# Attention scores as float32 products of 64 rows instead of products of split parts

## The chip, the cores and the metric

The kernel runs on one core of a Trainium2 chip. The metric is the time of one execution in device microseconds (us). A core has five engines that run side by side, each through its own list of instructions: TensorE (PE in the profile; its weight loads are PEld), VectorE (DVE), ScalarE (ACT), GpSimd (POOL) and SyncE (SP, which here only starts transfers). They wait for each other by semaphores. Products land in PSUM, eight banks of 512 float32 numbers on 128 partitions; PE, DVE and ACT reach it here.

## What is computed

Eight batches of eight heads, 576 tokens, 64 numbers per head. Half of the heads see a local window of 32 keys, the other half the keys at a distance of a multiple of 32. Then a feed-forward layer over all 4608 tokens, with weights that come as float64 numbers.

```python
scores = (1/8) * q @ k.T                     # per batch and head
rel = pos[:, None] - pos[None, :]
local   = (rel >= 0) & (rel < 32)            # heads 0 to 3
strided = (rel >= 0) & (rel % 32 == 0)       # heads 4 to 7
attn = softmax(where(mask, scores, -1e9))    # 1e-9 added to the sum
x = (attn @ v), heads side by side           # 4608 x 512
h = x @ w_in                                 # 512 x 2048
out = (h * clip(h + 3, 0, 6) / 6) @ w_out    # 2048 x 512
```

## The kernel before

**Pairs of heads.** Attention works on pairs of heads of one batch, 32 pairs in all, numbered 0 to 31 through the batches (four a batch: two local, two strided). The two heads of a pair lie on partitions 0 to 63 and 64 to 127 of one tile. A pair's steps are: load queries and keys (`qk`), transpose them by blocks on DVE (`t`), scores and softmax (`s`), transpose the probabilities and multiply by the values (`pv`), load the values (`v`).

**Blocks.** Local heads have six score blocks of 96 queries by 128 keys, strided heads five of 126 by 126; everything outside the blocks is masked anyway. So a local pair has 12 blocks and a strided pair 10.

**Two kinds of scores.** Pairs 0 to 7 (`PLAIN`) take the float32 transposes as they are and have float32 products (line 332): in pairs 0 to 3 over all 128 rows, with zeros in the place of the other head, in pairs 4 to 7 over the head's own 64 rows. These I call plain pairs. Pairs 8 to 31 split queries and keys in two float32r parts, a high part that ACT rounds (line 308) and a low part that DVE or POOL subtracts (line 309); DVE copies the keys' high part to the other half of the partitions (line 311). One product over 128 rows (line 334) then has the queries' high and low part against the keys' high part in its first columns and the high part against the keys' low part in the others. DVE adds the second columns to the mask (line 201), and then the first columns, with a running minimum (line 205). ACT takes the exponential (line 210), POOL divides by the sum (line 360).

**Banks.** A step of scores works on two blocks of one head and one bank, so a pair has six of them. Four banks (`w`) rotate among scores (`ps`), the second product of attention (`pv`) and the first product of the feed-forward (`ph`). The other four accumulate the second product of the feed-forward (`acc`).

**Second product of attention.** From pair 5 on DVE transposes the 32 by 32 blocks of the probabilities that can be other than zero (line 385), and line 411 multiplies, each head with 64 columns of the array.

**Feed-forward.** For each tile of 512 tokens and each of 16 chunks: 12 products into `ph` (lines 511 to 513), then ACT, DVE, ACT, POOL in a chain (lines 538, 539, 100, 101), and 12 products of the chunk before into `acc` (lines 494 to 496). The last 64 tokens of four batches make a tile of their own, `l`.

**Order.** The feed-forward of batch b is written with the attention steps of batch b + 1 spread evenly between its products; for the first two batches a string of steps gives the order. From that written order and a model of times a scheduler makes the list of each engine, with the chain at lines 538 to 101 at high priority. So a change of some steps moves other instructions too.

Of the kernel before, what the change touches and what calls it, by code (L numbers as in the profile page):

```python
# [8 lines left out]
F32 = mybir.dt.float32  # L9
# [18 lines left out]
NB = 3  # L28
VB = 1
PLAIN = 8  # L30
# [13 lines left out]
def attention_ffn(ctx: ExitStack, tc, q, k, v, w_in, w_out, out):  # L44
# [26 lines left out]
    # additive masks: local windows from PAD keys before the queries, strided blocks  # L71
# [19 lines left out]
    # They come as the words of float64 numbers (low, high) and are kept as two float32r parts, in  # L91
    # the same memory. The high word read as a float32 and scaled by 2**-112 has the float32
    # exponent and 20 bits of the mantissa three places to the right; the low word's top three
    # bits complete them.
# [8 lines left out]
    def weight_steps():  # L103
        """loads and conversions of parts of w_in (by rows) and w_out, in order of use"""
# [29 lines left out]
    def weights(loads, convs):  # L134
        """goes on to so many loads and conversions"""
        for todo, upto in ((wloads, loads), (wconvs, convs)):
            while todo and 8 * NQ - len(todo) < upto:
                todo.pop(0)()
# [6 lines left out]
    # the last tokens of four batches make a tile of their own  # L145
    left = [const.tile([P, NCC, B // 2 * LEFT], F32R, name=f"left{i}") for i in range(2)]

# [1 line left out]
    # Queries and keys come with 32 rows of tokens and half of a head's numbers on each quarter of  # L149
    # the partitions, so that transposes of 32 by 32 blocks give them by (head, number).  # L150
    # Scores of all but the first batches come from float32r parts: a head's queries' high part on
    # its own half of the partitions and the low part on the other, keys' high part on both beside
    # the low part on its own half. The first batches have float32 products.
    SR = [0, 7, 14, 21, STRIDE - RB]
    qk_plain, qk_split = [], []
# [12 lines left out]
    def split_k():  # L168
        if not qk_split:
            t = ap.tile([P, PAD + 4 * S], F32R, tag="kk", name="ksplit")  # L170
            nc.gpsimd.memset(t[:, :PAD].bitcast(F32), 0.0)
            for j in range(2):
                c0 = PAD + (2 * j + 1) * S
                nc.gpsimd.memset(t[D - D * j:P - D * j, c0:c0 + S].bitcast(F32), 0.0)
            qk_split.append(t)
        return qk_split[0]

    def keys(t, pad=0):
        """four parts of S keys; with pad, from so many columns before each part's first key"""
        return t[:, PAD - pad:PAD - pad + 4 * S].rearrange("p (a b s) -> p a b s", a=2, b=2)  # L180

    # probabilities of two heads, and their transposes, zero but for the 32 by 32 blocks that hold
    # allowed pairs
# [11 lines left out]
    def softmax(ps, mask, skip, e, mn, sm):  # L195
        """unnormalised exp of (ps + mask) over the last axis, into e; ps of several parts to add;
        the first block's first skip keys lie before all keys"""
        n, nb, w = e.shape
        m = mask.unsqueeze(1).to_broadcast([n, nb, w])
        if ps.shape[2] == 2:  # L200
            nc.vector.tensor_tensor(out=e, in0=ps[:, :, 1], in1=m, op=ALU.add)
            m = e
        for u in range(nb):
            c = slice(0 if u else skip, w)
            nc.vector.tensor_tensor_reduce(  # L205
                out=e[:, u, c], in0=ps[:, u, 0, c], in1=m[:, u, c], scale=-SCALE, scalar=BIG,
                op0=ALU.add, op1=ALU.min, accum_out=mn[:, u:u + 1])
# [8 lines left out]
    def bank(name):  # L216
        """a bank for what comes and goes; before the first tile those of the second product too"""
        nbank[0] += 1
        if before[0] and (early or nbank[0] % 2):
            acc = nbank[0] if early else nbank[0] // 2  # L220
            return pacc.tile([P, TOK], F32, tag=f"acc{acc % 4}", name=name)
        return pwk.tile([P, TOK], F32, tag="w", name=name)
# [41 lines left out]
    def pair_steps(b, c):  # L264
        """steps of one pair of heads: (loads, transposes, scores, probabilities, values)"""
# [11 lines left out]
        plain = b * NPAIR + c < PLAIN  # L277
# [17 lines left out]
        def t_split(x):  # L295
            def go():
                if x == "q":
                    d["qq"] = ap.tile([P, 2, S], F32R, tag="qq", name=f"qq{nm}")
                t = ap.tile([P, S], F32, tag="n", bufs=NB, name=f"{x}t{nm}")
                nc.vector.transpose(by_column(t), d[x])  # L300
                for j in range(2):
                    p, other = slice(D * j, D * j + D), slice(D - D * j, P - D * j)
                    if x == "q":
                        hi, lo = d["qq"][p, j], d["qq"][other, j]
                    else:
                        kt = keys(split_k())[:, j]
                        hi, lo = kt[p, 0], kt[p, 1]
                    nc.scalar.copy(hi, t[p])
                    (nc.vector, nc.gpsimd)[j if x == "q" else 1 - j].tensor_tensor(out=lo, in0=t[p], in1=hi.bitcast(F32), op=ALU.subtract)  # L309
                    if x == "k":  # L310
                        nc.vector.tensor_copy(kt[other, 0], hi.bitcast(F32))
            return go

        # score blocks of n queries and w keys; two share a bank
# [3 lines left out]
        k0 = q0 if loc else [x + PAD for x in q0]  # L318
        def s_step(j, i0):
            def go():  # L320
                blocks = range(i0, min(i0 + 2, nblk))
                ps = bank(f"ps{nm}{j}{i0}")
                np_ = 1 if plain else 2
                psv = ps[:n, :len(blocks) * np_ * w].rearrange("p (u t w) -> p u t w", u=len(blocks), t=np_)
                for u, i in enumerate(blocks):
                    pad = PAD if k0[i] < PAD else 0
                    kc = slice(k0[i] + pad - PAD, k0[i] + pad - PAD + w)
                    qc = slice(q0[i], q0[i] + n)
                    if plain:
                        own = slice(0, P) if padded else slice(D * j, D * j + D)  # L330
                        kt = keys(qk_plain[1], pad)[own, c % 2, j if padded else 0, kc]
                        nc.tensor.matmul(psv[:, u, 0], d["qt"][own, qc], kt, start=True, stop=True)
                    else:
                        nc.tensor.matmul(psv[:, u], d["qq"][:, j, qc], keys(split_k(), pad)[:, j, :, kc], start=True, stop=True)  # L334
                if i0 == 0:
                    if b * NPAIR + c < EARLY:
                        e = wp.tile([P, 6 * P], F32, tag=f"wo{NQ - 1}{c % 2 * 2 + j}", name=f"e{nm}{j}")
                    else:
                        if not es:
                            es.extend(ap.tile([P, 6 * P], F32, name=f"e{u}") for u in range(2))  # L340
                            for t in es:
                                nc.gpsimd.memset(t, 0.0)
                        e = es[j]
                    e = e[:, :nblk * P].rearrange("p (u w) -> p u w", u=nblk)
                    d["e", j] = e
                    if loc and b * NPAIR + c < EARLY:
                        nc.gpsimd.memset(e[:n, 0, :PAD], 0.0)
                    st = sp.tile([P, 2, 6], F32, tag="st", bufs=3, name=f"st{nm}{j}")
                    d["st", j] = st[:n, :, :nblk]
                e, st = d["e", j][:n, :, :w], d["st", j]  # L350
                sl = slice(i0, i0 + len(blocks))
                skip = PAD if loc and i0 == 0 else 0
                softmax(psv, mloc if loc else mstr, skip, e[:, sl], st[:, 0, sl], st[:, 1, sl])
                if i0 + 2 >= nblk:
                    sm = st[:, 1]
                    nc.vector.tensor_scalar_add(sm, sm, 1.0e-9)
                    nc.vector.reciprocal(sm, sm)  # L357
                    for bl, c0 in ((slice(0, 1), PAD), (slice(1, nblk), 0)) if loc else ((slice(0, nblk), 0),):
                        x = e[:, bl, c0:]
                        nc.gpsimd.tensor_tensor(out=x, in0=x, in1=sm[:, bl].unsqueeze(2).to_broadcast(x.shape), op=ALU.mult)  # L360
            return go

        where = {}

        def p_blocks(j):
            """transposes of the 32 by 32 blocks with allowed pairs"""
# [65 lines left out]
        ts = [(t_plain if plain else t_split)(x) for x in "qk"]  # L432
        ss = [s_step(j, i) for j in range(2) for i in range(0, nblk, 2)]
# [24 lines left out]
    def attention(b):  # L458
        """steps of one batch; the next pair's transposes stand between scores and probabilities"""
# [162 lines left out]
```

## Time and profile before

| | |
|---|---|
| runs | 1008.66 us median of 3 (1007.19 to 1011.6) |
| the profiled execution, first to last instruction | 1008.2 us |
| mean granted clock of TensorE | 0.978 of full speed |
| busy PE, DVE, ACT, POOL | 94%, 64%, 49%, 41% |
| transfers | 57.24 MB, most of it in the first 125 us |

In a row of grouped instructions stands the line, the engine, the operation, what is written and read, the shape, and the count. Behind it come the busy time, the mean duration in nanoseconds, and the idle time of the engine just before, with what ended it. A float32 product has two matmul records in the trace, a float32r product one. Durations of matmuls reach into each other, so what one adds is read from the starts. In a row of time order, "x4" says that four like records were merged, and the brackets give the idle time before and its end. "ps", "pv", "ph" and "acc" are the products named above, "ksplit" and "qq" the split keys and queries, "kplain" and "qplain" the plain ones.

### The profile page before, as it was taken

How to read it: one execution, taken by the hardware profiler on the slowest of the kernel's cores; microseconds unless marked ns; L12 is line 12 of the kernel's file. 1: busy time of each engine (PE TensorE's matmuls, PEld its weight loads, DVE VectorE, ACT ScalarE, POOL GpSimd, SP SyncE). 2: the span in 40 equal slices, each digit the busy share in tenths (PEclk: the TensorE clock that was granted, in tenths of full speed). 3: DMA queues.
4: the chain of work that ended last, by engine and by line, in shares of the span. 5: the costliest groups of instructions: out<-in, count | busy, mean ns of one | idle time of the engine just before them, and what ended most of it. 6: DMA issues, size and time to landing. Idle time of an engine off the chain costs nothing. (4 is left out here: it accounts for less than half of the span.)

```text
span 1008.2 us, 14965 instructions
## 1 busy us (share of the span) xinstructions
PE 948.7 (94%) x4848; PEld 765.7 (76%) x4848; DVE 648.0 (64%) x1869; ACT 489.3 (49%) x1346; POOL 412.2 (41%) x381
## 2 busy tenths in 40 slices
PE   5888898999999999999999999999899999999997
PEld 4665675778777778988787777778678878788896
DVE  7899999567777776126777777786766766311111
ACT  5676446455455444345554544555456445322232
POOL 4455566344434344225443444444434433222221
PEclk8898999899999999999999999999999999999999
DMA  7799400222222122103122311231213110100010
GB/s 149 160 283 295 91 14 16 58 61 37 37 58 63 30 38 45 43 1 60 34 38 46 77 27 36 38 79 27 41 32 77 33 25 14 42 1 1 1 42 21
DMA packets 207084, 57.24 MB, mean 57 GB/s; under 512 B 198304, under 2 KB 198304, under 8 KB 207008
## 3 DMA queue, kind: packets, MB, share of 16 engines
q1 hardware_dynamic: 207008, 56.31, 24.7%
q8 instruction: 38, 0.62, 0.3%
q14 instruction: 38, 0.31, 0.1%
HBM read 46.84 MB, written 9.44 MB: 56 GB/s over the span
## 5 line engine op out<-in xcount | busy, mean ns | idle before, releaser
L101 POOL TENSOR_TENSOR gl<-u,gh 128x512 fp32r<-128x512 f32 x128 | 170.4, 1333 | 241.8 <-ACT gh L100 223.3
L511 PE MATMUL ph<-xh,wi 128*128 128x512 f32 x512 | 209.4, 410 | 15.9 <-DVE u L539 8.2
L513 PE MATMUL ph<-xh,wi 128*128 128x512 f32 x512 | 205.0, 400 | 0.8 <-POOL wi L101 0.8
L512 PE MATMUL ph<-xl,wi 128*128 128x512 f32 x512 | 205.2, 401 | 0.4 <-DVE xl L428 0.4
L494 PE MATMUL acc<-wo,gh 128*128 128x512 f32 x512 | 201.9, 394 | 0.6 <-ACT gh L100 0.6
L495 PE MATMUL acc<-wo,gh 128*128 128x512 f32 x512 | 200.3, 391 | 0.0
L210 ACT ACTIVATE e<-e,st 126x126 f32<-126x126 f32 (+2 forms) x352 | 137.4, 392 | 92.2 <-DVE st L205 90.7
L496 PE MATMUL acc<-wo,gl 128*128 128x512 f32 x512 | 159.7, 395 | 0.0
L100 ACT CAST gh<-u 128x512 fp32r<-128x512 f32 x128 | 79.3, 619 | 161.6 <-DVE u L539 139.9
L539 DVE SCALAR_TENSOR_TENSOR u<-u,ph 128x512 f32<-128x512 f32 x128 | 86.4, 676 | 106.3 <-ACT u L538 105.5
L360 POOL TENSOR_TENSOR e<-e,st 96x96 f32<-96x96 f32 (+1 forms) x96 | 94.8, 1001 | 123.3 <-DVE st L357 104.3
L538 ACT ACTIVATE u<-ph,three 128x512 f32<-128x512 f32 x128 | 87.1, 681 | 92.7 <-PE ph L513 86.1
L511 PEld LDWEIGHTS ph<-xh,wi 128*128 128x128 f32 x512 | 98.6, 193 | 42.5 <-DVE u L539 11.0
L513 PEld LDWEIGHTS ph<-xh,wi 128*128 128x128 f32 x512 | 98.9, 193 | 23.4 <-POOL wi L101 1.4
L512 PEld LDWEIGHTS ph<-xl,wi 128*128 128x128 f32 x512 | 99.2, 194 | 19.5 <-DVE xl L428 1.3
L494 PEld LDWEIGHTS acc<-wo,gh 128*128 128x128 f32 x512 | 96.2, 188 | 21.5 <-ACT gh L100 1.2
L495 PEld LDWEIGHTS acc<-wo,gh 128*128 128x128 f32 x512 | 96.2, 188 | 18.2
L496 PEld LDWEIGHTS acc<-wo,gl 128*128 128x128 f32 x512 | 94.5, 188 | 20.3 <-POOL e L360 0.2
L385 DVE STREAM_TRANSPOSE atstr<-e 32x160 f32<-32x160 f32 x196 | 65.5, 334 | 8.4 <-POOL e L360 5.7
L205 DVE CUSTOM_DVE_ANT_0 e<-ps,e 96x128 f32<-96x128 f32 (+2 forms) x264 | 65.0, 280 | 2.4
L210 ACT ACTIVATION_READ_ACCUMULATOR e<-e,st 96x1 f32 (+1 forms) x352 | 66.2, 188 | 0.0
L385 DVE STREAM_TRANSPOSE atloc<-e 32x160 f32<-32x160 f32 (+1 forms) x156 | 56.5, 362 | 14.3 <-POOL e L360 12.3
(176 smaller groups left out, 1359.4 us busy)
## 6 DMA issues: line engine op xcount, KB each, us to landing
qn<-in_q_dram SPq DMA_DIRECT2D x128, 72.0 KB
kn<-in_k_dram SPq DMA_DIRECT2D x128, 72.0 KB
rawi<-in_moe_w_in_dram SPq DMA_DIRECT2D x16, 512.0 KB
rawo<-in_moe_w_out_dram SPq DMA_DIRECT2D x16, 512.0 KB
out_dram<-ob SPq DMA_DIRECT2D x32, 256.0 KB
vt<-in_v_dram SPq DMA_DIRECT2D x32, 160.0 KB
vt<-in_v_dram SPq DMA_DIRECT2D x160, 31.5 KB
out_dram<-obl SPq DMA_DIRECT2D x8, 128.0 KB
```

The lines of the kernel that those rows point to most:

```text
L101: eng.tensor_tensor(out=lo, in0=src, in1=hi.bitcast(F32), op=ALU.subtract)
L210: nc.scalar.activation(e[:, u, c], e[:, u, c], AF.Exp, bias=mn[:, u:u + 1], scale=-1.0, accum_out=sm[:, u:u + 1])
L360: nc.gpsimd.tensor_tensor(out=x, in0=x, in1=sm[:, bl].unsqueeze(2).to_broadcast(x.shape), op=ALU.mult)
L385: nc.vector.transpose(at[ks, i0:, qs], e[qs, i0:, ks])
L494: nc.tensor.matmul(acc[i], gh[:, sl], woh, start=fc == 0, stop=False)
L495: nc.tensor.matmul(acc[i], gh[:, sl], wol, start=False, stop=False)
L496: nc.tensor.matmul(acc[i], gl[:, sl], woh, start=False, stop=last)
L511: nc.tensor.matmul(ph, wih, xh[:, c], start=c == 0, stop=False)
L512: nc.tensor.matmul(ph, wih, xl[:, c], start=False, stop=False)
L513: nc.tensor.matmul(ph, wil, xh[:, c], start=False, stop=c == NCC - 1)
L538: nc.scalar.activation(u, ph, AF.Relu, bias=three)
L539: nc.vector.scalar_tensor_tensor(out=u, in0=u, scalar=6.0, in1=ph, op0=ALU.min, op1=ALU.mult)
```

## The change

All pairs are now like the plain ones 4 to 7 (pairs 0 to 3 stay over 128 rows). The split is gone, with its copies, subtractions and the addition at line 201. Query and key tiles of two pairs in turn lie in the two halves of the plain tiles. The first eight pairs (`FIRST`) keep their six score steps. From pair 8 on, four steps take their place: the first four blocks of both heads, in turn, into two banks and the softmax of the first head; the softmax of the second head; and the same for the remaining one or two blocks of each head. Comments that fell away are left out of the diff.

```diff
-PLAIN = 8
+FIRST = 8
...
     def softmax(ps, mask, skip, e, mn, sm):
         n, nb, w = e.shape
         m = mask.unsqueeze(1).to_broadcast([n, nb, w])
-        if ps.shape[2] == 2:
-            nc.vector.tensor_tensor(out=e, in0=ps[:, :, 1], in1=m, op=ALU.add)
-            m = e
         for u in range(nb):
             c = slice(0 if u else skip, w)
             nc.vector.tensor_tensor_reduce(
-                out=e[:, u, c], in0=ps[:, u, 0, c], in1=m[:, u, c], scale=-SCALE, scalar=BIG,
+                out=e[:, u, c], in0=ps[:, u, c], in1=m[:, u, c], scale=-SCALE, scalar=BIG,
...
-        def t_split(x):
-            def go():
-                if x == "q":
-                    d["qq"] = ap.tile([P, 2, S], F32R, tag="qq", name=f"qq{nm}")
-                t = ap.tile([P, S], F32, tag="n", bufs=NB, name=f"{x}t{nm}")
-                nc.vector.transpose(by_column(t), d[x])
-                for j in range(2):
...
-                    nc.scalar.copy(hi, t[p])
-                    (nc.vector, nc.gpsimd)[j if x == "q" else 1 - j].tensor_tensor(out=lo, in0=t[p], in1=hi.bitcast(F32), op=ALU.subtract)
-                    if x == "k":
-                        nc.vector.tensor_copy(kt[other, 0], hi.bitcast(F32))
-            return go
...
+        def scores(ps, j, i):
+            pad = PAD if k0[i] < PAD else 0
+            kc = slice(k0[i] + pad - PAD, k0[i] + pad - PAD + w)
+            own = slice(0, P) if padded else slice(D * j, D * j + D)
+            kt = keys(qk_plain[1], pad)[own, c % 2, j if padded else 0, kc]
+            nc.tensor.matmul(ps, d["qt"][own, q0[i]:q0[i] + n], kt, start=True, stop=True)
...
+        def s_both(i0, i1):
+            got = []
+            def mm():
+                blocks = range(i0, i1)
+                for j in range(2):
+                    ps = bank(f"ps{nm}{j}{i0}")
+                    got.append(ps[:n, :len(blocks) * w].rearrange("p (u w) -> p u w", u=len(blocks)))
+                for u, i in enumerate(blocks):
+                    for j in range(2):
+                        scores(got[j][:, u], j, i)
+                probabilities(got[0], 0, blocks)
+            def rest():
+                probabilities(got[1], 1, range(i0, i1))
+            return [mm, rest]
...
-        ts = [(t_plain if plain else t_split)(x) for x in "qk"]
-        ss = [s_step(j, i) for j in range(2) for i in range(0, nblk, 2)]
+        ts = [t_plain(x) for x in "qk"]
+        if b * NPAIR + c < FIRST:
+            ss = [s_step(j, i) for j in range(2) for i in range(0, nblk, 2)]
+        else:
+            ss = s_both(0, 4) + s_both(4, nblk)
```

What the scheduler makes of it is seen at two places. The first is TensorE's list at pair 13 (batch 3, a local pair; the digits in `ps_110` are the pair of the batch, the head, and the first block). Before, a stretch of products of one head stands between feed-forward products, here with two of the six steps (`ps_102` and `ps_114`) left out:

```order
L513 MATMUL ph_3_3105<-xh_1877,wi_580 128x512
L334 MATMUL ps_100_3156<-ksplit,qq_1_3018 96x256 x2
L494 MATMUL acc_0_2971<-wo_704,gh_2_3072 128x512
...
L494 MATMUL acc_2_2973<-wo_742,gh_3_3141 128x512
L334 MATMUL ps_104_3186<-ksplit,qq_1_3018 96x256 x2
L495 MATMUL acc_2_2973<-wo_742,gh_3_3141 128x512
...
L334 MATMUL ps_110_3211<-ksplit,qq_1_3018 96x256 x2
L334 MATMUL ps_112_3226<-ksplit,qq_1_3018 96x256 x2
L496 MATMUL acc_3_2974<-wo_742,gl_3_3142 128x512
```

Now (line 289 is the new place of line 332, lines 483 to 485 and 500 to 502 those of 494 to 496 and 511 to 513):

```order
L485 MATMUL acc_2_2884<-wo_704,gl_2_2951 128x512
L289 MATMUL ps_100_3034<-kplain,qplain 96x128
L289 MATMUL ps_110_3035<-kplain,qplain 96x128
...
L483 MATMUL acc_3_2885<-wo_704,gh_2_2950 128x512
...
L502 MATMUL ph_4_3056<-xh_1860,wi_902 128x512
L289 MATMUL ps_104_3078<-kplain,qplain 96x128 x2
L483 MATMUL acc_0_2882<-wo_742,gh_3_3019 128x512
...
L483 MATMUL acc_1_2883<-wo_742,gh_3_3019 128x512
L289 MATMUL ps_114_3079<-kplain,qplain 96x128 x2
L484 MATMUL acc_1_2883<-wo_742,gh_3_3019 128x512
```

The two rows ahead of the first "..." alternate four times, so eight blocks of both heads stand together; the last two blocks of each head stand in a place of their own, not beside the other head's.

The second place is DVE's list behind pair 12, from its softmax to that of pair 13 (`qq_1`, `ps_100` belong to pair 13, `qn_2` to pair 14). Before:

```order
L385 STREAM_TRANSPOSE atloc_1215<-e_1037 32x6x32 x4
L309 TENSOR_TENSOR qq_1_3018<-qt_1_3019,qq_1_3018 64x576
L385 STREAM_TRANSPOSE atloc_1215<-e_1037 32x6x32
L309 TENSOR_TENSOR ksplit<-kt_1_3034,ksplit 64x576
L311 CAST ksplit<-ksplit 64x576
L356 TENSOR_SCALAR st_01_2959<-st_01_2959 96x6
L300 STREAM_TRANSPOSE qt_2_3260<-qn_2_3049 128x18x32
L357 RECIPROCAL st_01_2959<-st_01_2959 96x6
L539 SCALAR_TENSOR_TENSOR u_2_3071<-u_2_3071,ph_2_3042 128x512
...
L201 TENSOR_TENSOR e_1037<-ps_100_3156,mloc 96x256
L205 ISA e_1037,st_10_3159<-ps_100_3156,e_1037 96x96
```

Now (lines 371, 528, 190 are 385, 539 and 205 of before; 272 and 276 are the transposes of queries and keys):

```order
L272 STREAM_TRANSPOSE qplain<-qn_2_2920 128x18x32
L276 STREAM_TRANSPOSE kplain<-kn_2_2925 128x18x32
...
L528 SCALAR_TENSOR_TENSOR u_1_2900<-u_1_2900,ph_1_2886 128x512
L371 STREAM_TRANSPOSE atloc_1215<-e_1037 32x5x32
L371 STREAM_TRANSPOSE atloc_1215<-e_1037 32x6x32 x5
...
L528 SCALAR_TENSOR_TENSOR u_2_2949<-u_2_2949,ph_2_2930 128x512
...
L190 ISA e_1037,st_10_3044<-ps_100_3034,mloc 96x96
```

The subtractions and the copy between the transposes of the probabilities are gone, and so is the addition ahead of the reductions.

More of the change, by code (lines that the diff above doesn't have):

```diff
@@ L154, in attention_ffn @@
     SR = [0, 7, 14, 21, STRIDE - RB]
-    qk_plain, qk_split = [], []
+    qk_plain = []
     def plain_q():
@@ L166, in plain_q @@
         return qk_plain[0]
[L168 to L171, printed above, removed]
-            for j in range(2):
[L173 to L176, printed above, removed]
     def keys(t, pad=0):
@@ L275, in vals @@
             d["v"] = load_v(b, c)
-        plain = b * NPAIR + c < PLAIN
         padded = b * NPAIR + c < KP
@@ L293, in t_plain @@
             return go
-        def t_split(x):
-            def go():
-                if x == "q":
-                    d["qq"] = ap.tile([P, 2, S], F32R, tag="qq", name=f"qq{nm}")
-                t = ap.tile([P, S], F32, tag="n", bufs=NB, name=f"{x}t{nm}")
-                nc.vector.transpose(by_column(t), d[x])
[L301 to L309, printed above, removed]
-                    if x == "k":
-                        nc.vector.tensor_copy(kt[other, 0], hi.bitcast(F32))
-            return go
         nblk = S // QB if loc else len(SR)
@@ L318, in pair_steps, with probabilities @@
         k0 = q0 if loc else [x + PAD for x in q0]
+        def scores(ps, j, i):
[4 more added lines that the diff above has]
+            nc.tensor.matmul(ps, d["qt"][own, q0[i]:q0[i] + n], kt, start=True, stop=True)
+        def probabilities(psv, j, blocks):
+            i0 = blocks[0]
+            if i0 == 0:
+                if b * NPAIR + c < EARLY:
+                    e = wp.tile([P, 6 * P], F32, tag=f"wo{NQ - 1}{c % 2 * 2 + j}", name=f"e{nm}{j}")
+                else:
+                    if not es:
+                        es.extend(ap.tile([P, 6 * P], F32, name=f"e{u}") for u in range(2))
+                        for t in es:
+                            nc.gpsimd.memset(t, 0.0)
+                    e = es[j]
+                e = e[:, :nblk * P].rearrange("p (u w) -> p u w", u=nblk)
+                d["e", j] = e
+                if loc and b * NPAIR + c < EARLY:
+                    nc.gpsimd.memset(e[:n, 0, :PAD], 0.0)
+                st = sp.tile([P, 2, 6], F32, tag="st", bufs=3, name=f"st{nm}{j}")
+                d["st", j] = st[:n, :, :nblk]
+            e, st = d["e", j][:n, :, :w], d["st", j]
+            sl = slice(i0, i0 + len(blocks))
+            skip = PAD if loc and i0 == 0 else 0
+            softmax(psv, mloc if loc else mstr, skip, e[:, sl], st[:, 0, sl], st[:, 1, sl])
+            if sl.stop == nblk:
+                sm = st[:, 1]
+                nc.vector.tensor_scalar_add(sm, sm, 1.0e-9)
+                nc.vector.reciprocal(sm, sm)
+                for bl, c0 in ((slice(0, 1), PAD), (slice(1, nblk), 0)) if loc else ((slice(0, nblk), 0),):
+                    x = e[:, bl, c0:]
+                    nc.gpsimd.tensor_tensor(out=x, in0=x, in1=sm[:, bl].unsqueeze(2).to_broadcast(x.shape), op=ALU.mult)
         def s_step(j, i0):
@@ L322, in go @@
                 ps = bank(f"ps{nm}{j}{i0}")
-                np_ = 1 if plain else 2
-                psv = ps[:n, :len(blocks) * np_ * w].rearrange("p (u t w) -> p u t w", u=len(blocks), t=np_)
+                psv = ps[:n, :len(blocks) * w].rearrange("p (u w) -> p u w", u=len(blocks))
                 for u, i in enumerate(blocks):
[L326 to L360, printed above, removed]
@@ L361, in s_step @@
-            return go
+                    scores(psv[:, u], j, i)
+                probabilities(psv, j, blocks)
+            return go
+        def s_both(i0, i1):
[12 more added lines that the diff above has]
+            return [mm, rest]
@@ L431, in pair_steps @@
         step = QB if loc else SB
-        ts = [(t_plain if plain else t_split)(x) for x in "qk"]
-        ss = [s_step(j, i) for j in range(2) for i in range(0, nblk, 2)]
+        ts = [t_plain(x) for x in "qk"]
+        if b * NPAIR + c < FIRST:
+            ss = [s_step(j, i) for j in range(2) for i in range(0, nblk, 2)]
+        else:
+            ss = s_both(0, 4) + s_both(4, nblk)
         groups = ([0, 1, 2], [3, 4, 5]) if loc else ([0, 1, 2, 3], [4])
```

## The prediction

> **What bounds the kernel now.** I read the page's engine row first, then the table of windows in three stretches (the start until the plain pairs are through, the stretch in which attention and feed-forward run side by side, and the tail), and then PE's waits in the second one. The columns of the table are length, busy time with instruction count of PE, PEld, DVE, ACT and POOL, then the granted clock and the DMA share.
>
> ```profile
> PE 948.7 (94%) x4848; PEld 765.7 (76%) x4848; DVE 648.0 (64%) x1869; ACT 489.3 (49%) x1346; POOL 412.2 (41%) x381
> 0.00:160.00 160.00, 129.08 (x683) 97.00 (x684) 145.85 (x371) 95.25 (x288) 85.84 (x93) 0.93 0.65 158
> 160.00:866.00 706.00, 683.16 (x3476) 552.73 (x3476) 481.84 (x1460) 353.21 (x982) 294.01 (x257) 0.99 0.20 41
> 866.00:1008.20 142.20, 136.50 (x693) 115.97 (x690) 20.36 (x38) 40.86 (x77) 32.37 (x32) 0.99 0.06 19
> ```
>
> The edited pairs, 8 to 31, all have their scores in the second stretch. PE, busy for 94% of the whole span, is busy there for 683.16 of 706 us, DVE for 481.84. The idle rest of PE is 706.00 - 683.16 = 22.84 us. The clock of 0.99 hides at most another 0.01 x 706 = 7 us of slow matmuls. So everything that PE could win from less loaded neighbours is about 30 us. What it waits for there, with total, count and longest:
>
> ```profile
> PE pv L411 <- issue: 9.6, 6, 2.2
> PE pv L411 <- DVE atloc L385: 5.5, 3, 2.5
> PE ph L511 <- DVE u L539: 5.1, 8, 3.6
> PE ph L511 <- DVE st L205: 1.7, 1, 1.7
> ```
>
> The reader is to see that all of it has DVE behind it: L411 needs DVE's block transposes L385, L511 a bank that DVE's L539 or L205 still reads. Even "issue" is such a case, as here, where PE idles 2.18 us until DVE's seven transposes end at 361.87 + 2.42 = 364.29:
>
> ```profile
> 361.87 2.42 DVE L385 STREAM_TRANSPOSE atstr<-e 32x160 f32<-32x160 f32 x7
> 364.39 0.52 PE L411 MATMUL pv<-atstr,vt 126*64 126x126 f32 x4 [2.18 <-issue]
> ```
>
> **What the change takes away.** These rows of the groups by shape name all of it (count, busy time, mean ns, idle time before):
>
> ```profile
> L309 POOL TENSOR_TENSOR ksplit<-kt,ksplit 64x576 fp32r<-64x576 f32 x24 | 36.7, 1529 | 64.4 <-ACT ksplit L308 36.1 <-PE ps L334 20.9 <-ACT gh L100 7.4
> L309 POOL TENSOR_TENSOR qq<-qt,qq 64x576 fp32r<-64x576 f32 x24 | 34.4, 1434 | 16.8 <-ACT qq L308 14.0 <-POOL e L360 1.6 <-POOL ksplit L309 0.8
> L311 DVE CAST ksplit<-ksplit 64x576 fp32r<-64x576 f32 x48 | 34.9, 728 | 2.8 <-ACT ksplit L308 1.2
> L308 ACT CAST ksplit<-kt 64x576 fp32r<-64x576 f32 x48 | 32.1, 669 | 12.2 <-PE ps L334 12.0
> L308 ACT CAST qq<-qt 64x576 fp32r<-64x576 f32 x48 | 32.1, 669 | 3.3 <-PE ps L334 1.9 <-PE ps L332 0.7
> L201 DVE TENSOR_TENSOR e<-ps,mloc 96x256 f32<-96x256 f32 x72 | 28.9, 418 | 30.3 <-PE ps L334 29.5
> L309 DVE TENSOR_TENSOR ksplit<-kt,ksplit 64x576 fp32r<-64x576 f32 x24 | 25.0, 1040 | 0.7
> L309 DVE TENSOR_TENSOR qq<-qt,qq 64x576 fp32r<-64x576 f32 x24 | 23.4, 976 | 1.1 <-ACT qq L308 0.4
> L201 DVE TENSOR_TENSOR e<-ps,mstr 126x252 f32<-126x252 f32 x48 | 19.7, 415 | 15.4 <-PE ps L334 15.0
> L201 DVE TENSOR_TENSOR e<-ps,mstr 126x126 f32<-126x126 f32 x24 | 6.9, 286 | 18.2 <-PE ps L334 18.1
> ```
>
> POOL loses 36.7 + 34.4 = 71 us, ACT 32.1 + 32.1 = 64, DVE 34.9 + 25.0 + 23.4 + 28.9 + 19.7 + 6.9 = 139. The transposes of queries and keys (L300, now as in L288 and L292) and the reductions L205 keep their number and size. None of these three engines sets the end, so the 274 us count only through the 30 us that PE waits. DVE's share in the stretch falls from 482 to about 343 of 706 us. I take 18 us as won back, three fifths: the waits behind a plain queue on DVE shrink, but the second product still stands behind softmax, POOL's multiplication and the transposes, and each score step now asks for two banks at once where it asked for one. The ends are 0 and 30.
>
> **What it adds to PE.** This is the term that decides. PE's rows, with start and duration: an old block of scores, a stretch of one new-style block (L332 has the same shapes in pairs 4 to 7), one of two blocks, and one in which blocks of both heads met. "xN" counts records; an L332 block has two of them, an L334 block one.
>
> ```profile
> 189.17 0.39 PE L495 MATMUL acc<-wo,gh 128*128 128x512 f32 x1
> 189.40 0.40 PE L334 MATMUL ps<-ksplit,qq 128*96 128x256 f32 x2
> 189.64 0.63 PE L496 MATMUL acc<-wo,gl 128*128 128x512 f32 x2
> ...
> 166.79 0.40 PE L513 MATMUL ph<-xh,wi 128*128 128x512 f32 x1
> 167.12 0.48 PE L332 MATMUL ps<-kplain,qplain 64*126 64x126 f32 x2
> 167.53 0.50 PE L511 MATMUL ph<-xh,wi 128*128 128x512 f32 x1
> 167.86 0.40 PE L512 MATMUL ph<-xl,wi 128*128 128x512 f32 x1
> ...
> 146.77 0.39 PE L513 MATMUL ph<-xh,wi 128*128 128x512 f32 x1
> 147.08 0.70 PE L332 MATMUL ps<-kplain,qplain 64*126 64x126 f32 x4
> 147.71 0.50 PE L494 MATMUL acc<-wo,gh 128*128 128x512 f32 x1
> 148.05 0.39 PE L495 MATMUL acc<-wo,gh 128*128 128x512 f32 x1
> ...
> 157.50 0.40 PE L494 MATMUL acc<-wo,gh 128*128 128x512 f32 x1
> 157.73 0.40 PE L495 MATMUL acc<-wo,gh 128*128 128x512 f32 x1
> 158.06 0.71 PE L332 MATMUL ps<-kplain,qplain 64*126 64x126 f32 x6
> 158.70 0.51 PE L513 MATMUL ph<-xh,wi 128*128 128x512 f32 x1
> ```
>
> Durations of matmuls overlap, so I go by starts. A feed-forward matmul takes 157.73 - 157.50 = 0.23 us. Two old blocks take 189.64 - 189.40 = 0.24, or 0.12 each, and the matmul ahead of them keeps its 0.23: they cost nothing beside themselves. One new block makes 167.86 - 166.79 = 1.07, less two ordinary steps of 0.23 that is 0.61. Two make 148.05 - 146.77 = 1.28, less 0.46 that is 0.82. The difference of 0.21 is two records: 0.11 each, and 0.61 - 0.22 = **0.39 us is a fixed price of each stretch**, half of it on the way in (167.12 comes 0.33 after 166.79), half on the way out and behind (167.86 comes 0.33 after 167.53). Six records with blocks of both heads took 158.70 - 157.73 = 0.97, no more than four alone (147.71 - 146.77 = 0.94): two of the six ran beside two others.
>
> The fixed price has a rule beside it: the Trainium skill, "TensorEngine Tiling (Array Packing)", Tiling Modes, says that changing the tiling mode, not just the tile, drains TensorE. The rows agree: 64 of 128 rows cost 0.39 per stretch, the 128-row L334 nothing.
>
> Now the count, in the order of the changed program. A mid pair has eight alternating blocks in one stretch, then the rest of each head in a stretch of its own, where the scheduler found the second bank free only later. Over the 24 pairs there are 264 blocks as before, in 73 stretches. With each record beside the other head's where the order lets them stand together, the 528 records need 374 places of 0.11. That is 374 x 0.11 + 73 x 0.39 = 41.1 + 28.5 = 69.6 us, against 264 x 0.12 = 31.7 before: **+38 us**. The second product, 64 columns wide, enters and leaves the same way. It is now cut into 75 stretches instead of 57, which is at most 18 x 0.39 = 7 us, but its heads alternate in more of them. I take +3, with ends 0 and 7.
>
> Nothing on PE covers this: in the stretch it has only those 30 us free. The first 160 us hold only pairs that stay plain, and their order is the same; the tail has no attention. Loads of queries and keys find their tiles free earlier, which at a DMA share of 0.20 is worth nothing.
>
> **Sum.** The profiled execution spans 1008.2 us, 0.5 under the median of the runs (1008.66, from 1007.19 to 1011.6), so I add to it directly: 1008.2 + 38 + 3 - 18 = **1031 us**. With nothing won back it is 1049, with all 30 us 1019.
>
> **Rivals.**
> *Heads do not overlap.* The 158.06 row is the only meeting of two heads' scores; its blocks went to two banks, as they now always do, which speaks for overlap. Against it: the order sometimes puts three blocks of a head in a row, and a late bank would part the two. With every record alone PE needs 528 x 0.11 + 28.5 = 86.6, so +55, and 1008.2 + 55 + 3 - 18 = 1048 us.
> *The fixed price is lateness, not a switch.* Then DVE's relief decides, and the kernel gets faster. If the 0.33 us steps at 167.12 and 167.53 came from weights or banks that were not ready, the lighter program would not pay them. PE would add 41.1 - 31.7 = 9 us, and with 18 to 30 won back the end is 987 to 999. It decides from the point where a stretch costs under 0.39 - (41 - 18) / 91 = 0.14 us, over 73 + 18 stretches. For it: both examples stand near semaphore waits. Against it: the two stretches show the same 0.39 to 0.01 us, at different places and with different neighbours. A half-way case (0.08 to 0.19) ends within 0.5% of before. The same page of the Trainium skill (Overview) promises up to twice the speed for a contraction of 64 and less. Taken alone that would make 264 places of 0.11, 29 us, 3 less than before; the rows of 146.77 and 166.79 speak against its being the whole bill.
>
> **Chances.** Forecast 0.70; no overlap, or waits for two banks of the same size, 0.17; the price not paid, fully or by half, 0.13. A change of under about 0.5% (5 us) can't be told from none here: faster 0.06, same 0.07, slower 0.87. The likeliest case has 1019 to 1042; to hold eight in ten I reach up through the serial case and a little below the full win-back: 1016 to 1050.
>
> **What would show it.** In the new profile the score line should have 528 records of about 0.27 us on 64 rows, from pair 8 on, many starting within 0.01 us of another of the other head; the step into each stretch should be 0.33 us and not 0.23. PE's instruction count rises by 264. PE must stay above 95% busy between 160 us and the end of attention, with DVE under 50%, and that stretch must be longer by some 23 us while the first 160 us and the tail stay. If L411's waits on DVE are gone and the stretch is still longer, the terms are right. If PE's idle time grows past 30 us, banks are the cause that I underrated; if the steps into stretches are 0.23, the fixed price was wrong, and so is the sign.

## The result, and the profile after

The changed kernel takes **1022.4 us** (median of four runs, 1021.84 to 1024.39) against 1008.5 us in the same comparison: 1.0131 times the time before, 95% interval 1.0104 to 1.0157. It is slower, as forecast, by 14 us where the forecast had 22; the time lies in the stated range.

The profiled execution spans 1020.1 us. The page's engine row, and the windows in the same three stretches as before (the second ends with the last attention work, now about 876 us):

```profile
PE 977.9 (96%) x5112; PEld 764.1 (75%) x5112; DVE 509.5 (50%) x1629; ACT 430.5 (42%) x1250; POOL 335.5 (33%) x330
0.00:160.00 160.00, 127.24 (x670) 96.52 (x671) 147.34 (x365) 93.99 (x283) 83.91 (x92) 0.93 0.66 162
160.00:876.00 716.00, 712.30 (x3747) 550.14 (x3746) 342.71 (x1230) 295.46 (x892) 218.73 (x207) 1.00 0.19 40
876.00:1020.10 144.10, 138.36 (x699) 117.49 (x697) 19.49 (x35) 41.09 (x75) 32.86 (x32) 0.99 0.06 19
```

DVE, ACT and POOL lost about what was counted (DVE 648.0 to 509.5, ACT 489.3 to 430.5, POOL 412.2 to 335.5: 139, 59 and 77 us, for 139, 64 and 71). PE's records rose by 264 to 5112. In the middle stretch PE's idle time fell from 22.84 to 716.00 - 712.30 = 3.70 us, and the clock is full, but the stretch is 10 us longer (the prediction had some 23): PE has more to do, and nothing else sets the time there. What it still waits for in that window:

```profile
PE pv L397 <- DVE u L528: 1.5, 1, 1.5
PE ph L500 <- DVE u L528: 1.3, 1, 1.3
PE pv L397 <- DVE st L190: 0.6, 1, 0.6
PE acc L483 <- ACT gh L100: 0.3, 1, 0.3
```

Now PE's rows around pair 13 in time order, first the stretch with eight blocks of both heads in turn, then the two with the rest of each head:

```profile
322.47 0.39 PE L485 MATMUL acc<-wo,gl 128*128 128x512 f32 x1
322.79 1.12 PE L289 MATMUL ps<-kplain,qplain 64*96 64x128 f32 x16
323.83 0.50 PE L483 MATMUL acc<-wo,gh 128*128 128x512 f32 x1
324.17 0.40 PE L484 MATMUL acc<-wo,gh 128*128 128x512 f32 x1
...
327.18 0.39 PE L502 MATMUL ph<-xh,wi 128*128 128x512 f32 x1
327.50 0.67 PE L289 MATMUL ps<-kplain,qplain 64*96 64x128 f32 x4
328.10 0.50 PE L483 MATMUL acc<-wo,gh 128*128 128x512 f32 x1
328.44 0.40 PE L484 MATMUL acc<-wo,gh 128*128 128x512 f32 x1
```

The 16 records took 324.17 - 322.47 = 1.70, less two ordinary steps of 0.23 that is 1.24 us: eight places of 0.11 and 0.36. The four records of one head took 328.44 - 327.18 - 0.46 = 0.80: four places of 0.11 and 0.36. So both heads' records do run beside each other, and the second, short stretch pays a fixed price as large as that of the long one.

I summed this over all score stretches from pair 8 on, from the start of the matmul ahead to the second one behind, less two ordinary steps: 73 stretches, 528 records in 364 places, **67.0 us**. The 264 old blocks at 0.12 come to 31.7.

### The profile page after: what moved, and what is told of

Its sections match the earlier page's. It is cut to its first block, busy times and chain, and to the rows that moved or that the text cites. A ratio compares the mean times of both kernels' runs of the same rounds, so it can differ in the third digit from the quotient of the medians.

```text
span 1020.1 us, 15024 instructions
## 1 busy us (share of the span) xinstructions
PE 977.9 (96%) x5112; PEld 764.1 (75%) x5112; DVE 509.5 (50%) x1629; ACT 430.5 (42%) x1250; POOL 335.5 (33%) x330
## 4 chain that ended last, share of the span: by engine, by line
PE 83%; DVE 9%; SPq 4%; DMA 2%; ACT 1%; issue 1%; POOL 0%; DVEq 0%; ACTq 0%
PE acc L483 12%; PE ph L500 11%; PE acc L484 11%; PE acc L485 11%; PE ph L501 10%; PE ph L502 10%; PE ps L289 5%; PE pv L397 4%; SPq L224 2%; PE phl L500 1%; PE phl L502 1%; PE phl L501 1%; PE accl L483 1%; PE accl L484 1%; PE accl L485 1%; DVE fo L123 1%
## 5 line engine op out<-in xcount | busy, mean ns | idle before, releaser
L101 POOL TENSOR_TENSOR gl<-u,gh 128x512 fp32r<-128x512 f32 x128 | 168.2, 1315 | 443.6 <-ACT gh L100 414.3
L483 PE MATMUL acc<-wo,gh 128*128 128x512 f32 x512 | 207.6, 406 | 0.3 <-ACT gh L100 0.3
L484 PE MATMUL acc<-wo,gh 128*128 128x512 f32 x512 | 201.0, 393 | 0.0
L485 PE MATMUL acc<-wo,gl 128*128 128x512 f32 x512 | 174.2, 394 | 0.0
L500 PEld LDWEIGHTS ph<-xh,wi 128*128 128x128 f32 x512 | 96.8, 189 | 38.2 <-DVE u L528 5.0
L318 POOL TENSOR_TENSOR e<-e,st 96x96 f32<-96x96 f32 (+1 forms) x96 | 92.0, 976 | 79.7 <-DVE st L315 59.4
L502 PEld LDWEIGHTS ph<-xh,wi 128*128 128x128 f32 x512 | 97.6, 191 | 22.7 <-POOL wi L101 1.4
L289 PEld LDWEIGHTS ps<-kplain,qplain 64*96 64x96 f32 (+3 forms) x704 | 67.9, 180 | 45.9 <-issue 34.2
L289 PE MATMUL ps<-kplain,qplain 64*96 64x128 f32 (+3 forms) x704 | 87.6, 296 | 13.9 <-DVE kplain L276 10.7
L414 DVE TENSOR_TENSOR xl<-pv,xh 128x288 fp32r<-128x288 f32 (+1 forms) x64 | 33.4, 526 | 93.2 <-ACT xh L413 93.1
L190 DVE CUSTOM_DVE_ANT_0 e<-ps,mloc 96x96 f32<-96x96 f32 (+1 forms) x192 | 43.5, 276 | 71.9 <-PE ps L289 71.8
```

The costliest lines, as they stand in the source:

```text
L101: eng.tensor_tensor(out=lo, in0=src, in1=hi.bitcast(F32), op=ALU.subtract)
L289: nc.tensor.matmul(ps, d["qt"][own, q0[i]:q0[i] + n], kt, start=True, stop=True)
L483: nc.tensor.matmul(acc[i], gh[:, sl], woh, start=fc == 0, stop=False)
L484: nc.tensor.matmul(acc[i], gh[:, sl], wol, start=False, stop=False)
L485: nc.tensor.matmul(acc[i], gl[:, sl], woh, start=False, stop=last)
L500: nc.tensor.matmul(ph, wih, xh[:, c], start=c == 0, stop=False)
```

## The experiments

All times are medians. Each set was run beside the kernel before, whose medians were 1009.77, 1009.04 and 1010.44 us in the three sets; ratios are to it.

### The price of 64 rows against the price of float32

The first kernel has all pairs over 128 rows, with zeros in the place of the other head, as pairs 0 to 3 have it.

```diff
-KP = 4
+KP = 32
```

> Edit: all pairs lie as pairs 0 to 3 do, each head's queries and keys over 128 rows with zeros in the place of the other head; the products stay float32, the order of steps stays. Heads can no longer overlap. Theory (the fixed price of a stretch, 0.39 us, belongs to blocks on 64 of the 128 rows): no fixed price for scores, 528 records of 0.11 us one after the other, about 58 us in place of the 67 us that the changed kernel's trace shows for its score stretches, so about 9 us faster than the changed kernel, near 1013 us. Rival (the price belongs to the change between float32r and float32 products): 58 + 73 x 0.39 = 86 us, so about 19 us slower, near 1041 us. DVE gets one transpose of 1.0 us more per pair, 24 us in all, which should hide.

Measured: 1012.38 us, ratio 1.0030 (1.0011 to 1.0048). PE's rows, with the same four records of one head's last blocks:

```profile
324.06 0.39 PE L502 MATMUL ph<-xh,wi 128*128 128x512 f32 x1
324.29 0.60 PE L289 MATMUL ps<-kplain,qplain 128*96 128x128 f32 x4
324.64 0.49 PE L483 MATMUL acc<-wo,gh 128*128 128x512 f32 x1
324.97 0.39 PE L484 MATMUL acc<-wo,gh 128*128 128x512 f32 x1
```

324.97 - 324.06 - 0.46 = 0.45 us: four places of 0.11 and nothing besides; the step into the stretch is 0.23. The products are float32 and stand between float32r ones, so the type carries no price. Doubling the rows, half of them zeros, is 10 us faster than the changed kernel. From pair 8 on, the score stretches sum to 58 us in place of 67. The edit also pads pairs 4 to 7, and 1.8 of the 10 us stand already ahead of pair 8: the 351st feed-forward matmul, with 392 attention records ahead of it in both traces, starts at 179.0 us in place of 180.8. Whether that is the padding or a difference between two executions was not separated.

The reverse needs the type kept and the rows halved. The next two kernels start from the kernel before and leave out the low parts of queries and keys (their places hold zeros, so the scores are those of rounded numbers). The first shows the relief of DVE and POOL by itself, with PE's products as before; the second differs from it only in the rows.

```diff
                     nc.scalar.copy(hi, t[p])
-                    (nc.vector, nc.gpsimd)[j if x == "q" else 1 - j].tensor_tensor(out=lo, in0=t[p], in1=hi.bitcast(F32), op=ALU.subtract)
-                    if x == "k":
-                        nc.vector.tensor_copy(kt[other, 0], hi.bitcast(F32))
...
-                softmax(psv, mloc if loc else mstr, ...)
+                softmax(psv[:, :, :1], mloc if loc else mstr, ...)
```

> Edit: the kernel before, with the low parts of queries and keys left out: their halves are set to zero once, the subtractions, the copy of the keys' high part and the addition ahead of the reductions are gone, so the scores are products of the rounded high parts alone. PE has the same products as before. DVE loses about 139 us and POOL 71 us, ACT keeps its copies. Theory (the relief is worth the stalls of PE, some 23 of 27 us, less a few more stretches of the second product): about 18 to 22 us faster than before, near 988 us. Rival (DVE's relief is worth little, the changed kernel's gain came from elsewhere): within 5 us of before.

```diff
-                        nc.tensor.matmul(psv[:, u], d["qq"][:, j, qc], keys(split_k(), pad)[:, j, :, kc], start=True, stop=True)
+                        own = slice(D * j, D * j + D)
+                        nc.tensor.matmul(psv[:, u], d["qq"][own, j, qc], keys(split_k(), pad)[own, j, :, kc], start=True, stop=True)
```

> Edit: as the kernel with the low parts left out, but each product uses only the head's own 64 rows; still float32r, still one record of 256 columns per block. The rest is the same. Theory (the price belongs to 64 rows): the order has about 134 stretches of scores, so 134 x 0.39 = 52 us slower than the kernel with the low parts left out, near 1040 us, and steps of 0.33 us into each stretch. Rival (the price belongs to float32 beside float32r, or to lateness): no difference, near 988 us, steps of 0.23 us.

Measured: the relief alone 986.58 us, ratio 0.9764 (0.9725 to 0.9804); with 64 rows 1036.38 us, ratio 1.0258 (1.0216 to 1.0300). The window of the first from 160 us to the end of its attention shows where the relief went, 690.00 - 687.33 = 2.67 us of idle PE:

```profile
160.00:850.00 690.00, 687.33 (x3514) 554.28 (x3513) 353.04 (x1226) 355.55 (x991) 220.62 (x209) 1.00 0.21 43
```

A score stretch of the second in time order:

```profile
323.53 0.39 PE L512 MATMUL ph<-xh,wi 128*128 128x512 f32 x1
323.85 0.47 PE L333 MATMUL ps<-ksplit,qqhi 64*96 64x256 f32 x2
324.25 0.50 PE L510 MATMUL ph<-xh,wi 128*128 128x512 f32 x1
324.59 0.39 PE L511 MATMUL ph<-xl,wi 128*128 128x512 f32 x1
```

324.59 - 323.53 - 0.46 = 0.60 us, of which two places of 0.12; the rest, 0.36, is the fixed price, now with float32r throughout. The two kernels differ by 49.8 us; over 134 stretches that is 0.37 us each. With the rule of the Trainium skill, "TensorEngine Tiling (Array Packing)", Tiling Modes (a change of the tiling mode drains TensorE), this agrees: the price came with 64 rows in either type, and went with 128.

The weight loads (PEld) show what is late in such a step. Here is the first load of the stretch above, and below it that of the 128-row stretch at 324.29 us in the kernel with all pairs over 128 rows:

```profile
323.85 0.24 PEld L333 LDWEIGHTS ps<-ksplit,qqhi 64*96 64x96 f32 x2 [0.35 <-issue]
...
324.06 0.61 PEld L289 LDWEIGHTS ps<-kplain,qplain 128*96 128x96 f32 x4
```

The 64-row load starts together with its matmul (323.85), the 128-row load 0.23 us ahead of its own (324.06 against 324.29). From 200 us on this is so at each of the 131 entries into a score stretch of the 64-row float32r kernel, at each of the 69 of the changed kernel, and at each way out: 1 to 2 ns from the load's start to the matmul's, where the load of a 128-row stretch starts at least 0.22 us ahead. So the next weights are not loaded under the running matmul when the rows change. Whether PE drains, or only holds the load back, these rows do not separate.

### What taking both heads in turn is worth

```diff
-FIRST = 8
+FIRST = 32
```

> Edit: the changed kernel, but all pairs keep the six score steps of one head each, two blocks in one bank; 64 rows, float32. Heads hardly meet. Theory (0.39 us per stretch plus 0.11 us per record that runs alone): the order has 135 stretches of scores, so 528 x 0.11 + 135 x 0.39 = 58 + 53 = 111 us in place of 67, about 43 us slower than the changed kernel, near 1065 us. Rival (taking both heads in turn is worth little, the loss came from the new order and the banks): within 10 us of the changed kernel.

Measured: 1066.14 us, ratio 1.0560 (1.0508 to 1.0612). So with 64 rows, the steps of both heads together save 44 us against the old steps. The sum over its stretches, made as above, is 135 stretches, 528 places, 110.5 us against 67.0: 164 places more, at 0.11 some 18 us, are the overlap that is lost, and the rest goes with 62 stretches more.

### Half rows where the heads meet, whole rows elsewhere

This and the last kernel keep the keys padded, and use 64 rows only for the four alternating blocks.

```diff
-KP = 4
+KP = 32
...
-            own = slice(0, P) if padded else slice(D * j, D * j + D)
+            own = slice(0, P) if padded and not half else slice(D * j, D * j + D)
...
-                        scores(got[j][:, u], j, i)
+                        scores(got[j][:, u], j, i, half=i0 == 0)
```

> Edit: keys with zeros for the other head as in the 128-row kernel, but the first four blocks of both heads use 64 rows, in turn, and the remaining one or two blocks of each head use all 128 rows. Theory (0.39 us only for stretches with 64-row blocks, records of both heads overlap only there): in the order 42 us of places, and 32 stretches with the price (106 of both kinds less 74 of the second product), 42 + 32 x 0.39 = 55 us in place of 67, so about 12 us faster than the changed kernel, near 1010 us. Rival (overlap is worth nothing beyond the price): as the 128-row kernel or slower, 1012 us and more.

Measured: 1008.00 us, ratio 0.9989 (0.9966 to 1.0012): 14 us faster than the changed kernel, and no difference from before that can be told. Its score stretches sum to about 54 us in place of 67; here too pairs 4 to 7 are padded.

### The same price in the second product

The second product uses 64 of the array's 128 columns, and a row of the changed kernel's trace has its fixed price too:

```profile
314.53 0.39 PE L484 MATMUL acc<-wo,gh 128*128 128x512 f32 x1
314.85 0.38 PE L397 MATMUL pv<-atloc,vt 128*64 128x96 f32 x2
315.16 0.50 PE L500 MATMUL ph<-xh,wi 128*128 128x512 f32 x1
315.50 0.39 PE L501 MATMUL ph<-xl,wi 128*128 128x512 f32 x1
```

One block alone: 315.50 - 314.53 - 0.46 = 0.51 us. The scheduler often lets the first head's first block run ahead by itself, since the other head's transposes come later. Taking the second head first holds the block back until both are there.

```diff
-                    for j in range(2):
+                    for j in (1, 0):
                         a = where[j, i][:, skip:]
```

> Edit: in the changed kernel the second product of attention takes the pair's second head first, so that its first matmul waits for the later of the two sets of transposes and the rest can follow at once. Theory (a stretch of 64-column matmuls has the same fixed price as one of 64-row blocks): the order has 58 stretches of the second product in place of 75 and 78 of scores in place of 73, and about 3 us fewer places; 17 x 0.39 + 3 - 5 x 0.39 = 8 us faster than the changed kernel, near 1014 us, if PE's waits for the transposes do not grow. Rival (columns have no such price): 3 us faster at most.

> Edit: the same turn of the two heads in the second product, in the kernel before. Theory: the order has 30 stretches of the second product in place of 57 and about 8 us fewer places; 27 x 0.39 + 8 = 19 us faster than before if PE's waits stay, near 990 us; they may grow by some us, since PE then waits with less behind it. Rival (columns have no such price): 8 us faster at most.

Measured: 1020.63 us in the changed kernel, ratio 1.0120 (1.0093 to 1.0147), and 1007.39 us in the kernel before, ratio 0.9987 (0.9972 to 1.0003). Both expectations missed: 2 us where 8 were expected, and under 2 where 19 were. In the kernel before, the stretches did shrink. Their sum from 186 us on fell from 69.0 us in 56 stretches (waits inside them counted) to 35.4 in 30. But a new wait took most of the gain. The next feed-forward product may have been placed for an earlier end of its chain, which no run shows; PE's waits in the middle window:

```profile
PE acc L494 <- ACT gh L100: 26.0, 21, 3.4
PE acc L496 <- POOL gl L101: 0.7, 4, 0.2
```

In the changed kernel the same wait stands in the first 190 us, in the window from 60 us on:

```profile
PE acc L483 <- ACT gh L100: 12.3, 4, 5.2
PE acc L485 <- POOL gl L101: 2.3, 3, 1.0
```

By the work done, PE is 2.7 us behind there: the 401st feed-forward matmul, with 432 attention records ahead of it in both traces, starts at 200.8 us in place of 198.1. The granted clock between 100 and 135 us is lower too, 0.80 in place of 1.00, so waits and slow matmuls were not told apart. From there to the end the turned kernel wins back 5 us. So the turn was tried from pair 8 on only:

```diff
+                    for j in ((1, 0) if b * NPAIR + c >= 8 else (0, 1)):
```

> Edit: the changed kernel, with the heads of the second product turned only from pair 8 on. Theory (a stretch of 64-column matmuls costs 0.39 us): 60 stretches in place of 75, 2.8 us fewer places, and 78 stretches of scores in place of 73; 15 x 0.39 + 2.8 - 5 x 0.39 = 7 us faster than the changed kernel, near 1015.5 us. Rival (columns have no such price): 2 us faster at most.

Measured: 1017.90 us, ratio 1.0085 (1.0056 to 1.0114), 4.5 us faster than the changed kernel, between theory and rival. The stretches of the second product, 57 in place of 73 behind the first tile, sum to 45.8 in place of 54.1 us, and the score stretches rose from 67.0 to 69.9: 5.4 us less in all. The profiled execution is shorter by only 3.4 us: it is 1.9 us late already at its 51st feed-forward matmul (71.5 against 69.6 us), ahead of every pair that the edit turns, so that difference is not the edit's. The two turned kernels differ in the first eight pairs alone, and in time by 1020.63 - 1017.90 = 2.7 us. The gain of 8.3 us in the product itself holds places and stretches together, so a price per column stretch is only read from rows like the one above: 0.51 less two places of 0.08, about 0.35 us. The 0.08 is estimated from the last kernel below, where a stretch with four places more takes 0.33 us more from its first start to that of the next matmul.

### All of it together

```diff
+                ps = None
                 for j in range(2):
-                    ps = bank(f"ps{nm}{j}{i0}")
-                    got.append(ps[:n, :len(blocks) * w].rearrange("p (u w) -> p u w", u=len(blocks)))
+                    if i0 == 0 or ps is None:
+                        ps = bank(f"ps{nm}{j}{i0}")
+                    c0 = 0 if i0 == 0 else j * len(blocks) * w
+                    got.append(ps[:n, c0:c0 + len(blocks) * w].rearrange("p (u w) -> p u w", u=len(blocks)))
```

This is added to half rows where the heads meet and to the turned heads: the last blocks of both heads now share one bank. First with the heads turned in all pairs, then from pair 8 on.

> Edit: the kernel with 64 rows for the first four blocks and 128 for the rest, with the heads of the second product turned, and the last blocks of both heads in one bank. Theory: 25 us of places and 50 stretches for the second product (44.5 us in place of 58.8), 43 us of places and 33 stretches for scores (56 us in place of 67), so about 25 us faster than the changed kernel, near 997 us. Rival (columns have no such price): the scores' 11 us and 3 us of places, near 1008 us.

> Edit: the kernel with half rows first, last blocks of both heads in one bank and the heads of the second product turned, but turned only from pair 8 on. Theory (the turned heads in the first eight pairs cost the 9.7 us by which their first tile ended later, 203.7 against 194.0 us; from there on stretches cost 0.39 us each): 51 stretches of the second product and 34 of 64-row scores as before, the first tile back at about 194 us, near 997 us. Rival (the turn itself costs waits anywhere, the first pairs are no special place): within 3 us of 1005.65.

Measured: 1005.65 us, ratio 0.9969 (0.9953 to 0.9984), and **997.59 us**, ratio 0.9879 (0.9849 to 0.9909). The second is faster than the kernel before and than the changed kernel. These two combined kernels differ only in the turn in the first eight pairs, which is the 8 us between them: at the 401st feed-forward matmul the first is 8.1 us behind (204.2 against 196.1 us, 432 attention records ahead in both). (The 203.7 and 194.0 us of the last expectation are the starts of the first copy out of the first tile's banks, in the first of these and in the changed kernel, and not the tile's end.) The windows of the second up to and past the middle stretch:

```profile
160.00:852.00 692.00, 687.04 (x3729) 550.97 (x3730) 365.05 (x1243) 292.14 (x887) 216.43 (x205) 1.00 0.20 41
852.00:996.30 144.30, 138.36 (x699) 117.50 (x697) 19.56 (x35) 41.21 (x75) 32.95 (x32) 1.00 0.06 19
```

The score stretches sum to 55.2 us and those of the second product to 42.1, against 67.0 and 54.1 in the changed kernel: 24 us, as the time has it (1022.4 - 997.6 = 25). What the shared bank is worth was not run alone. Against the kernel with half rows where the heads meet (1008.00 us), the gain of 10 us is found in the second product (some 55 to 42 us); its scores, at about 54 us, were no longer than these.

## Why the prediction was right

**The sign and its reason** were right. PE set the time of the middle stretch, the 274 us taken from the other engines counted only through PE's waits, and the fixed price of a stretch was real.

**Scores on PE:** +38 was forecast, 67.0 - 31.7 = +35 came. The count of stretches (73) was exact. 364 places came for 374 counted, so the order was read as costing a little more than it did. The fixed price was 0.36 to 0.39 us. Float32 and float32r at 64 rows have it and both at 128 rows do not, so it belongs to the rows.

**Second product:** +3 was forecast, from 57 to 75 stretches. The sum over them is 58.8 us after. Before, waits stand inside them, so the clean sum is only estimated, at some 55 from the same places and price: no contradiction, but not a measurement either.

**Won back from waits:** this was the term that was mis-sized. 18 us of 30 were forecast as won back, "three fifths", on the ground that the second product would still stand behind softmax and transposes and that each step would want two banks. PE's idle time fell by 22.84 - 3.70 = 19.1 us, and the clock rose from 0.99 to 1.00. Gap by gap (each start beyond its ordinary step, slow-clock matmuls too) the lost time from 170 us on was 27.3 us before and is 4.1 now: 23. The kernel with the relief alone agrees: 23 us faster than before, with 2.67 us of idle PE left. Nearly all waits went; neither reason for holding back showed.

**The rest.** 35 + 3 - 23 = +15, and the span rose by 11.9, the median by 13.9. The two misses, 3 us in the scores and 5 in the waits, go the same way, so none hides the other. The 3 us between sum and span were not traced; the estimate for the second product alone could hold them.

**Rivals.** *Heads do not overlap* fell: 528 records took 364 places. The kernel with the heads apart needed all 528; of its 44 us some 18 are the overlap. *The fixed price is lateness* fell: it is there in every quoted 64-row stretch, with no wait for another engine in the row, and in none of the 128-row ones. The weight load is late, but it is so at every entry and way out, which a tile or bank that happened not to be ready would not be. The "up to twice" for a short contraction of the Trainium skill, "TensorEngine Tiling (Array Packing)", Overview, holds for the eight alternating blocks themselves (16 records in eight places), but not for the stretch, which pays 0.36 us for 0.88 of work.

## What to carry to other kernels

Read the price of a short matmul from the start of the one ahead to the second one behind: what a block on part of the array costs is mostly in its neighbours. If the array is otherwise used whole, gather such blocks in few and long stretches, or fill the other half with zeros when only a few stand together. Where an engine that is not the bound is relieved, the most it can give is the bound engine's idle and slow-clock time; here that was nearly all given, and it was less than what the bound engine was asked to do more.

## What the runs showed that was not expected

Zeros in the other 64 rows (1012.38 us) beat two heads side by side in 64 rows each (1022.4 us), with 58 us of places against 67.0 us of places and prices. And a rule that holds a block back, so that a stretch is whole, took 8 us out of the second product in the middle of the program, of which the longer score stretches took 3 back. At the start of the program the same rule cost 2.7 us in the changed kernel and 8 in the combined one, where PE then waited for the feed-forward's chain on ACT.
